# A linear-attention block: the state product by single heads on four 32-column tiles of TensorE

## The chip, the cores and the metric

One core of one Trainium2 chip. The time is the device time of one execution of the whole program, in microseconds; the figure for a kernel is the median of its runs.

## The reference

One transformer block on x of 2048 tokens by 640, all in 32 bits, with scale, shift and gate rows from a condition vector c (`mod = silu(c) @ w_mod`, six rows of 640). What matters here is its first half, attention with 32 heads of 20:

```python
q, k, v = split(h @ wqkv)                      # h: layer norm of x, scaled and shifted
phi(p) = concat(softmax(p @ w_phi), softmax(-p @ w_phi))        # per head, 20 + 20 features
kv  = einsum("bhsf,bhsd->bhfd", phi_k, v)      # the state: 40 x 20 a head, summed over all tokens
z   = einsum("bhsf->bhf", phi_k)               # the sums of k
num = einsum("bhqf,bhfd->bhqd", phi_q, kv)
den = einsum("bhqf,bhf->bhq", phi_q, z) + 1e-6
x   = x + ga * ((num / den) @ wo)
```

The second half is a layer norm and an MLP of 640 by 1728 with squared ReLU, and a second gated residual.

## The kernel before

Tokens are cut into 16 tiles of 128 (`NT`), taken in pairs `j` of 256. Nearly every product of the block is made in three terms of rounded operands (`three`: high by high, high by low, low by high), so a projection of one token tile to 640 columns is 30 matmuls of 128 by 128 by 320 elements. Products whose operands are plain 32-bit numbers, the state product among them, show in the trace as two weight loads and two matmuls each.

*First phase.* `first` folds `w_phi` into the weights of q and k, makes the first modulation rows (`mod_rows2`, line 530: a product with 32 equal columns a tile of the array, on four column tiles) and the first two tiles. Then a loop over t = 2 to 13 runs, for each token tile: `proj("k")`, `do_v`, `do_q`, the softmax numerators (`spread`, `exps`), the norm of k (`k_norm`), the sums of the numerators of q (`q_sums`, `q_chain`), and `do_kv(t - 1)`. `t1` transposes the next pair's normalized tokens for the projections through PSUM banks. `ln_parts` is the layer norm of a later pair, on ScalarE and GpSimd. The order on TensorE is the order written (`by_pe`); on the other engines a planner puts the instructions in order by its estimate of time, and each engine then runs its list in order. `sides` is work that the second half needs: modulation rows (`mod_rows`, `mod_cols`: loads, five multiply-adds on VectorE, then matmuls or transposes) and the output weights (`prep_wo`), advanced by two steps a tile and by eight from t = 11.

*The state.* `do_kv` takes the 32 heads in 11 groups `UN` of three heads (the last of two). The value tile of a group is stationary, 60 columns and one column of ones, so that the state and the sums of k come out together; the features of k stream, 2 x 60 elements. Groups alternate between two 64-column tiles of the array. Each product also holds the cross terms of its three heads, which a mask takes away later. The state lies in a PSUM tile `kvp` of three banks; its third bank and the tile `tp` also serve transposes and small products.

*Between the phases* everything is in the order written on TensorE, VectorE, ScalarE and GpSimd (`order`). The last four token tiles' q is postponed to here as cover (`POSTPONED`). The state is copied to SBUF (`kvs`); `make_z` spreads the sums of k over all partitions with products against a column of the identity (line 735), and copies them to `zb`. From `zb` the denominators follow on VectorE and GpSimd (`e_prod`: lines 831 and 833; `e_recip`; `e_scale`: lines 852 and 857), and `tr_e` transposes the scaled features (line 978). `kv_diags` and `kv_masks` transpose the state and mask it for the first four pairs' `num`; `kv2_mask`, `kv2_pick` and `kv2_turn` make a second arrangement of it for the later pairs. A loop over `j` in 0 to 3 then does the output product (`do_wo`), with jobs hung in at places `EXTRA[(j, place)]`: `ln_next`, `blocks` and `back` (a transpose of blocks through DRAM), `turn` (line 1190), and `both`.

*Second phase.* `group(g)` runs the MLP over groups of 512 tokens: `up_mm`, `up_relu` (line 1394), `up_out`, `down`. MLP weights are loaded and split in high and low by `prep_load`, `prep_hi` (line 1093) and `prep_lo`, in the order `preps`; raw weights wait in rows tagged "s1" (three buffers) up to index 8, then "s1", "s2", "s4" in turn. The later half of the tokens' attention output is filled in behind the MLP of the first two groups.

Of the kernel before, what the change touches and what calls it, by code (L numbers as in the profile page):

```python
# [15 lines left out]
P = 128  # L16
# [11 lines left out]
UN = [(60 * u, 60) for u in range(10)] + [(600, 40)]  # L28
NU = len(UN)
# [14 lines left out]
def kernel(  # L44
# [80 lines left out]
    kvp = psK.tile([P, 3, 512], F32, name="kvp")  # L125
# [22 lines left out]
    vt = [pc.tile([P, NU, 64], F32, name=f"vt{i}") for i in range(2)]  # L148
    mask2 = pc.tile([120, 128], F32, name="mask")
    mask = mask2[:, :64]  # L150
    mask5 = pc.tile([80, 40], F32, name="mask5")
    for v in vt:
        nc.gpsimd.memset(v, 0.0)
        nc.gpsimd.memset(v[:, :, 60:61], 1.0)

    def head_mask(m, rows, n, at):

        m3 = m.rearrange("p (h d) -> p h d", d=DH)
        nc.gpsimd.affine_select(out=m3, in_=m3, compare_op=ALU.is_ge, fill=0.0, base=-at,
                                pattern=[[-DH, n], [0, DH]], channel_multiplier=1)  # L160
        nc.gpsimd.affine_select(out=m3, in_=m3, compare_op=ALU.is_ge, fill=0.0, base=DH - 1 + at,
                                pattern=[[DH, n], [0, DH]], channel_multiplier=-1)

    mtmp = row("s2", "mtmp")[:120, :60]
    nc.gpsimd.memset(mask, 0.0)
    nc.gpsimd.memset(mask[:, :60], 1.0)
    nc.gpsimd.memset(mtmp, 1.0)
    head_mask(mask[:, :60], 120, 3, 0)
    head_mask(mtmp, 120, 3, 60)
    nc.gpsimd.tensor_tensor(mask[:, :60], mask[:, :60], mtmp, op=ALU.add)  # L170
    nc.gpsimd.tensor_copy(mask2[:, 64:], mask)
    nc.gpsimd.memset(mask5, 1.0)
    nc.gpsimd.memset(mtmp[:80, :40], 1.0)
    head_mask(mask5, 80, 2, 0)
    head_mask(mtmp[:80, :40], 80, 2, 40)
    nc.gpsimd.tensor_tensor(mask5, mask5, mtmp[:80, :40], op=ALU.add)


# [80 lines left out]

    def to_cols(acc, dest, nm):  # L260
        ps = [(0, 4, tp(f"mc{nm}")), (4, 1, kvp[:, 2])]
# [23 lines left out]
    def mod_cols(part, dest):  # L285
# [3 lines left out]
        yield  # L289
        yield  # L290
# [3 lines left out]
    def mod_rows(part, dest):  # L294
        for acc in mod_acc(part):
            if acc is None:
                yield
        yield
        yield
        for h in range(2):  # L300
            p = kvp[:, 2] if h else tp(f"mr{part}")
            nc.tensor.matmul(p[:, :HALF], ones, acc[:, h * HALF : (h + 1) * HALF], start=True, stop=True)
            nc.scalar.activation(dest[:, h * HALF : (h + 1) * HALF], p[:, :HALF], AF.Copy)
        yield
# [65 lines left out]
    def t1(j, ds):  # L370
# [3 lines left out]
        for d in ds:  # L374
            b = banks.setdefault(d // 2, kvp[:, 2] if d // 2 == 1 else tp(f"ta{j}_{d}"))
            t_in(XB[j], d, b[:, 256 * (d % 2) : 256 * (d % 2) + 256])
        for d in ds:
            t_out(cols_a, HT[j], d, f"a{j}", banks[d // 2][:, 256 * (d % 2) : 256 * (d % 2) + 256])
# [15 lines left out]
    def do_v(t):  # L394
        p = proj("v", t, ((0, 360), (360, 640)))
        v = vt[t % 2]
        nc.scalar.activation(v[:, 0:6, :60], p[0][:, :360].rearrange("p (g d) -> p g d", d=60), AF.Copy)
        nc.scalar.activation(v[:, 6:10, :60], p[1][:, :240].rearrange("p (g d) -> p g d", d=60), AF.Copy)
        nc.scalar.activation(v[:, 10, :40], p[1][:, 240:280], AF.Copy)
# [22 lines left out]
    def do_kv(t):  # L422
        v, e = vt[t % 2], EK[t]
        for u, (o, n) in enumerate(UN):
            g, c = divmod(u, 2)
            a = 120 * (g % 4)
            nc.tensor.matmul(  # L427
                kvp[64 * c : 64 * c + 64, g // 4, a : a + 2 * n].rearrange("p (s n) -> p s n", s=2),
                v[:, u], e[:, :, o : o + n],
                start=(t == 0 and g % 4 == 0), stop=(t == NT - 1), skip_group_check=True,  # L430
            )
# [47 lines left out]
    def side():  # L479
        ga_b = row("s4", "ga_b")  # L480
        yield from mod_rows(2, ga_b)
        for g in range(NG):
            yield from prep_wo(g, ga_b)
            yield
# [10 lines left out]
    sides = side()  # L495
# [22 lines left out]
    def half(b, h):  # L518
        return kvp[:, b, 256 * h : 256 * h + 256]
# [131 lines left out]
    do_kv(0)  # L651
# [3 lines left out]
    layer1(2)  # L655
    for t in range(2, NT - 2):
# [22 lines left out]
        if not i and turns:  # L679
            t1(j + 1, turns)  # L680
# [8 lines left out]
    for _ in sides:  # L689
        pass  # L690
# [24 lines left out]
    nc.scalar.activation(kvs[:, :480], kvp[:, 0, :480], AF.Copy)  # L715
    nc.scalar.activation(kvs[:, 480:600], kvp[:, 1, :120], AF.Copy)
    nc.scalar.activation(kvs[:64, 600:680], kvp[:64, 1, 120:200], AF.Copy)
# [10 lines left out]
    kv5 = kv_t[:80, 640:760]  # L728
    def make_z():
        for c in range(2):  # L730
            for b, (g0, g1) in enumerate(((0, 4), (4, 6 - c))):
                r = P if c else 64
                a, n = 480 * b, ((480, 200), (480, 120))[c][b]
                p = psA.tile([P, 512], F32, tag="pj", name=f"z{c}_{b}", bufs=4)
                nc.tensor.matmul(p[:, :n], ident[:r, 64 * c + 60 : 64 * c + 61].to_broadcast([r, P]),
                                 kvs[:r, a : a + n], start=True, stop=True)
                m = min(g1, 5) - g0
                for h in range(2):
                    dst = zb[:, h, 120 * g0 : 120 * (g0 + m)].rearrange("p (g c n) -> p g c n", c=2, n=60)[:, :, c]
                    src = p[:, : 120 * m].rearrange("p (g s n) -> p g s n", s=2, n=60)[:, :, h]  # L740
                    if h:
                        nc.vector.tensor_copy(dst, src)
                    else:
                        nc.scalar.activation(dst, src, AF.Copy)
                if g1 == 6:
                    nc.vector.tensor_copy(zb[:, :, 600:640], p[:, 120:200].rearrange("p (s n) -> p s n", s=2))
# [3 lines left out]
    kvt = [None, None]  # L750
# [1001 lines left out]
```

## Time and profile before

| | |
|---|---|
| median of 3 runs | 780.5 us (780.25 to 781.21) |
| profiled execution | 780.53 us, its span 778.8 us |
| TensorE busy | 770.5 us, 99% of the span; weight loads 716.1 us |
| VectorE, ScalarE, GpSimd busy | 552.7, 401.5, 77.5 us |
| granted TensorE clock | full in all 40 slices |
| moved by DMA | 142.31 MB, 183 GB/s over the span |

Matmuls overlap and their ends are modelled, so the busy share of TensorE does not say that it works at its peak; the time from one matmul's start to the next tells more, and the chain of waits tells which engine sets the end in each stage. "PEld" is TensorE's weight load.

### The profile page before, as it was taken

How to read it: one execution, taken by the hardware profiler on the slowest of the kernel's cores; microseconds unless marked ns; L12 is line 12 of the kernel's file. 1: busy time of each engine (PE TensorE's matmuls, PEld its weight loads, DVE VectorE, ACT ScalarE, POOL GpSimd, SP SyncE). 2: the span in 40 equal slices, each digit the busy share in tenths (PEclk: the TensorE clock that was granted, in tenths of full speed). 3: DMA queues.
4: the chain of work that ended last, by engine and by line, in shares of the span. 5: the costliest groups of instructions: out<-in, count | busy, mean ns of one | idle time of the engine just before them, and what ended most of it. 6: DMA issues, size and time to landing. Idle time of an engine off the chain costs nothing.

```text
span 778.8 us, 13323 instructions
## 1 busy us (share of the span) xinstructions
PE 770.5 (99%) x5163; PEld 716.1 (92%) x5163; DVE 552.7 (71%) x917; ACT 401.5 (52%) x789; POOL 77.5 (10%) x181
## 2 busy tenths in 40 slices
PE   9999999999999999999999999999999999999997
PEld 8899999999999988898999999998999999989997
DVE  4499979998888488573968799958935252575544
ACT  4677585765753235755957345332366545433221
POOL 3002000100100112201323010100010000000000
PEclk9999999999999999999999999999999999999999
DMA  9614215634223263467799657996679754145121
GB/s 346 257 35 133 102 69 188 235 103 154 87 86 103 86 205 137 156 204 269 258 307 351 213 194 244 259 369 191 174 245 365 272 171 147 60 142 203 38 82 68
DMA packets 76437, 142.31 MB, mean 183 GB/s; under 512 B 12718, under 2 KB 37422, under 8 KB 76374
## 3 DMA queue, kind: packets, MB, share of 16 engines
q1 hardware_dynamic: 69094, 117.41, 46.2%
q0 software_dynamic: 4096, 16.78, 5.8%
q10 hardware_dynamic: 3184, 7.27, 2.6%
q8 instruction: 40, 0.66, 0.4%
q14 instruction: 23, 0.19, 0.1%
HBM read 98.40 MB, written 42.93 MB: 181 GB/s over the span
## 4 chain that ended last, share of the span: by engine, by line
PE 84%; DVE 6%; DMA 4%; ACT 3%; POOL 2%; issue 1%; SPq 0%; ACTq 0%; DVEq 0%; POOLq 0%
PE up L70 22%; PE acc L70 14%; PE acr L70 9%; PE pv L70 9%; PE pk L70 9%; PE pq L70 8%; PE pwo L70 4%; PE kvp L427 3%; DVE dn L833 1%; DVE scr L831 1%; DMA rw<-in_w 1%; DVE ezb L852 1%; DMA xb<-in_x 1%; DMA sb<-xn 1%; PE foldq L242 1%
## 5 line engine op out<-in xcount | busy, mean ns | idle before, releaser
L70 PE MATMUL up<-h,w 128*128 128x512 f32 (+1 forms) x910 | 197.8, 370 | 1.1 <-ACT r L1394 0.9
L70 PEld LDWEIGHTS up<-h,w 128*128 128x128 f32 x910 | 155.5, 188 | 28.8 <-DVE h L80 1.2
L70 PE MATMUL acc<-w,r2t 128*128 128x384 f32 x656 | 150.7, 336 | 0.0
L70 PE MATMUL acr<-w,r2t 128*128 128x256 f32 x656 | 112.8, 279 | 0.0
L70 PEld LDWEIGHTS acc<-w,r2t 128*128 128x128 f32 x656 | 107.5, 188 | 4.2 <-DVE w L80 0.2
L70 PEld LDWEIGHTS acr<-w,r2t 128*128 128x128 f32 x656 | 105.5, 188 | 0.0
L70 PE MATMUL pwo<-wo,ot 128*128 128x320 f32 (+1 forms) x512 | 79.5, 313 | 0.2 <-DVE xm L1063 0.2
L70 PEld LDWEIGHTS pwo<-wo,ot 128*128 128x128 f32 (+1 forms) x512 | 75.8, 188 | 1.1 <-DVE xm L1063 0.4
L70 PE MATMUL pk<-wk,hT 128*128 128x320 f32 x480 | 75.3, 313 | 0.0
L70 PE MATMUL pq<-wq,hT 128*128 128x320 f32 x480 | 74.0, 311 | 0.4 <-ACT k L403 0.4
L70 PE MATMUL pv<-wv,hT 128*128 128x360 f32 (+1 forms) x480 | 72.8, 309 | 0.0
L70 PEld LDWEIGHTS pk<-wk,hT 128*128 128x128 f32 x480 | 70.6, 188 | 1.8 <-issue 0.6
L70 PEld LDWEIGHTS pv<-wv,hT 128*128 128x128 f32 x480 | 71.5, 188 | 0.0
L70 PEld LDWEIGHTS pq<-wq,hT 128*128 128x128 f32 x480 | 70.6, 188 | 0.9 <-ACT k L403 0.6
L1394 ACT ACTIVATE r<-up,b_t 128x512 f32<-128x512 f32 x52 | 35.0, 680 | 66.9 <-PE up L70 58.9
L80 DVE TENSOR_TENSOR r2t<-r,r2t 128x512 fp32r<-128x512 f32 (+1 forms) x56 | 38.3, 685 | 33.0 <-ACT r2t L1406 30.1
L1405 DVE TENSOR_TENSOR r<-r 128x512 f32<-128x512 f32 x26 | 17.9, 690 | 47.1 <-ACT r L1394 47.1
L80 DVE TENSOR_TENSOR w<-rw,w 128x640 fp32r<-128x640 f32 (+2 forms) x42 | 33.3, 813 | 24.4 <-ACT w L1093 12.9
L1406 ACT ACTIVATE r2t<-r 128x512 fp32r<-128x512 f32 x52 | 32.9, 633 | 22.5 <-DVE r L1405 21.6
L1496 ACT ACTIVATE w<-rw 128x640 fp32r<-128x640 f32 x42 | 30.6, 729 | 26.4 <-DVE rw L1495 24.1
L403 ACT ACTIVATE q<-pq 128x320 f32<-128x320 f32 x32 | 13.8, 438 | 31.5 <-PE pq L70 30.9
L403 ACT ACTIVATE k<-pk 128x320 f32<-128x320 f32 x32 | 13.5, 431 | 29.5 <-PE pk L70 29.4
(248 smaller groups left out, 1078.1 us busy)
## 6 DMA issues: line engine op xcount, KB each, us to landing
rw<-in_w SPq DMA_DIRECT2D x65, 320.0 KB, 3.5
w<-w2d SPq DMA_DIRECT2D x28, 320.0 KB, 4.7
w<-w1d SPq DMA_DIRECT2D x12, 640.0 KB, 6.3
esp<-eq SPq DMA_DIRECT2D x11, 640.0 KB, 4.7
wm<-in_w_mod SPq DMA_DIRECT2D x20, 320.0 KB, 3.6
xb<-in_x SPq DMA_DIRECT2D x8, 640.0 KB, 4.4
el<-esp SPq DMA_DIRECT2D x8, 640.0 KB, 5.4
xx<-in_x SPq DMA_DIRECT2D x16, 320.0 KB, 5.5
```

Of the source, the lines that this page charges most:

```text
L70: nc.tensor.matmul(o, a, b, start=first and i == 0, stop=last and i == len(terms) - 1, skip_group_check=skip,)
L80: (eng or nc.vector).tensor_tensor(out_lo, full, hi.bitcast(F32), op=ALU.subtract)
L242: nc.tensor.matmul(p[g // 3][:, (g % 3) * 120 : (g % 3) * 120 + n], r, bd_t[:n, g * 120 : g * 120 + n], start=True, stop=True,)
L403: nc.scalar.activation(t[:, h * HALF : (h + 1) * HALF], p[h][:, :HALF], AF.Copy)
L427: nc.tensor.matmul(kvp[64 * c : 64 * c + 64, g // 4, a : a + 2 * n].rearrange("p (s n) -> p s n", s=2), v[:, u], e[:, :, o : o + n], start ...
L831: nc.vector.tensor_tensor(z, flat(ET[t]), flat(zb), op=ALU.mult)
L833: nc.vector.tensor_reduce(dn.rearrange("p s h -> p (s h)"), heads(z), axis=AX.X, op=ALU.add)
L852: nc.vector.tensor_tensor(EU[t][:, :1200].rearrange("p (u s h d) -> p s u h d", s=2, h=3, d=DH), ET[t][:, :, :600].rearrange("p s (u h d) ...
L1394: nc.scalar.activation(r, UP[f], AF.Relu, bias=b1_t[:, f : f + 1])
L1405: nc.vector.tensor_tensor(r, r, r, op=ALU.mult)
L1406: nc.scalar.activation(t[:, 0], r, AF.Copy)
L1496: nc.scalar.activation(w[:, 0], raw, AF.Copy)
```

## The change

1. `do_kv` takes single heads: the value tile is 32 columns a head (20 values, one column of ones, the rest zeros), 2 x 20 features stream, and the heads go round the four 32-column tiles of the array. No cross terms arise. The state then fills 360 columns of one PSUM bank instead of 680 in two; `kvp` becomes three separate tiles.
2. `make_z` uses four products, each of 32 rows of the array (four row groups), into four banks. The state is transposed in three blocks instead of six, once for each arrangement. The masks become one number a partition and head, made on GpSimd; one masked product on VectorE (`masked`) repeats a head's state three times.
3. In the loop `do_kv(t - 2)` stands behind the k projection of tile t, where `do_kv(t - 1)` stood at the end; `t1` follows it, three column blocks on even tiles and two on odd ones, before `do_v`. Side work is in two lists, `mods` and `wos`; the matmuls of `mods` wait for an odd tile and stand behind `t1`.
4. `v` is cut 320 and 320, with two copies to SBUF instead of three; modulation rows are cut 384 and 256.
5. The second arrangement's picks move from place (2, 2) to (2, 1), its turn from (3, 2) to (2, 3); `prep_load` puts the raw rows 5 to 8 in "s4".

```diff
-    kvp = psK.tile([P, 3, 512], F32, name="kvp")
+    kvp = [psK.tile([P, 512], F32, name=f"kvp{b}") for b in range(3)]
...
+    def head_mask(m, rows, n, step):
+
+        tmp = mtmp[:rows, :n]
+        nc.gpsimd.memset(m, 0.0)
+        for at in rows_of(n, step):
+            nc.gpsimd.memset(tmp, 1.0)
+            nc.gpsimd.affine_select(out=tmp, in_=tmp, compare_op=ALU.is_ge, fill=0.0, base=-at,
+                                    pattern=[[-step, n]], channel_multiplier=1)
+            nc.gpsimd.affine_select(out=tmp, in_=tmp, compare_op=ALU.is_ge, fill=0.0, base=step - 1 + at,
+                                    pattern=[[step, n]], channel_multiplier=-1)
+            nc.gpsimd.tensor_tensor(m, m, tmp, op=ALU.add)
...
     def do_v(t):
-        p = proj("v", t, ((0, 360), (360, 640)))
...
+        p = proj("v", t)
+        for h in range(2):
+            nc.scalar.activation(vt[t % 2][:, 16 * h : 16 * h + 16, :DH], heads(p[h][:, :HALF]), AF.Copy)
...
     def do_kv(t):
         v, e = vt[t % 2], EK[t]
-        for u, (o, n) in enumerate(UN):
-            g, c = divmod(u, 2)
-            a = 120 * (g % 4)
-            nc.tensor.matmul(
-                kvp[64 * c : 64 * c + 64, g // 4, a : a + 2 * n].rearrange("p (s n) -> p s n", s=2),
-                v[:, u], e[:, :, o : o + n],
-                start=(t == 0 and g % 4 == 0), stop=(t == NT - 1), skip_group_check=True,
-            )
+        for g in range(9):
+            for c in range(4 if g < 6 else 3 if g < 8 else 2):
+                b, i = divmod(g, 3)
+                h, o = 12 * b + 3 * c + i, state(c, b)
+                nc.tensor.matmul(
+                    o[32 * c : 32 * c + 32, :, i], v[:, h], heads4(e)[:, :, h],
+                    start=(t == 0 and g == 0), stop=(t == NT - 1), skip_group_check=True,
+                )
...
+    def sides(n):
+        for _ in range(n):
+            if not held[0]:
+                held[0] = next(mod_steps, "end")
+            elif gated[0]:
+                next(wo_steps, None)
...
     q_chain(0)
-    do_kv(0)
...
+    head_mask(mask_b, P, 3, DH // 4)
+    head_mask(mask5_b, P, 2, DH // 4)
     for t in range(2, NT - 2):
...
-        turns = ((0, 1) if i == 0 else (2, 3, 4)) if j + 1 < NT // 2 else ()
-        if turns and t == NT - 3:
-            t1(j + 1, turns)
+        do_kv(t - 2)
+        if j + 1 < NT // 2 and t > 2:
+            t1(j + 1, (3, 4) if i else range(3))
+        if i and held[0] == "pe":
+            held[0] = next(mod_steps)
+            gated[0] = True
         do_v(t)
+        if t == 2:
+            t1(j + 1, range(3))
...
-        if i and turns and t < NT - 3:
-            t1(j + 1, turns)
...
-        do_kv(t - 1)
-        for _ in range(SIDES[t >= RAWQ]):
-            next(sides, None)
+        sides(SIDES[t >= RAWQ])
...
         to_sb(proj("k", t), PK[t])
+        do_kv(t - 2)
...
-    do_kv(ka - 1)
...
+        ps = [bank("z0"), bank("z1"), bank("z2"), psA.tile([P, 512], F32, tag="pj", name="z3", bufs=4)]
+        for c, p in enumerate(ps):
+            r, n = slice(32 * c, 32 * c + 32), (360, 360, 320, 240)[c]
+            nc.tensor.matmul(p[:, :n], ident[r, 32 * c + DH : 32 * c + DH + 1].to_broadcast([32, P]), kvs[r, :n], start=True, stop=True)
+        for c, p in enumerate(ps):
+            dst = zb[:, :, :480].rearrange("p s (b c n) -> p s b c n", c=4, n=60)[:, :, :, c]
+            put(c % 2, dst, p[:, :240].rearrange("p (b s n) -> p s b n", s=2, n=60))
...
     def kv_diags():
-        kvt[:] = [bank(f"kvt{b}") for b in range(2)]
-        for g in range(5):
...
+        p = KV1["p"] = bank("kvt")
+        for b in range(3):
+            nc.tensor.transpose(p[:120, P * b : P * b + P], kvs[:, 120 * b : 120 * b + 120], ident)
...
-        raw = row(("s1", "s2", "s4")[i % 3] if i > 8 else "s1", f"rw{k}_{f}")
+        raw = row(("s1", "s2", "s4")[i % 3] if i > 8 else "s4" if i > 4 else "s1", f"rw{k}_{f}")
...
-        (2, 1): [lambda: ln_next(1)],
-        (2, 2): [lambda: ln_next(1), lambda: ln_next(1), kv2_mask, kv2_pick],
+        (2, 1): [lambda: ln_next(1), kv2_pick],
+        (2, 2): [lambda: ln_next(1), lambda: ln_next(1)],
...
-        (2, 3): [lambda: back(1)],
+        (2, 3): [kv2_turn, lambda: back(1)],
...
-        (3, 2): [kv2_turn, lambda: (p_hi(), p_lo()), lambda: turn(1)],
+        (3, 2): [lambda: (p_hi(), p_lo()), lambda: turn(1)],
```

More of the change, by code (lines that the diff above doesn't have):

```diff
@@ L147 @@
     rs_q = pc.tile([P, NTA, 2 * H], F32, name="rs_q")
[L148 to L151, printed above, removed]
+    vt = [pc.tile([P, H, 32], F32, name=f"vt{i}") for i in range(2)]
+    mask = pc.tile([120, 3], F32, name="mask")
+    mask5 = pc.tile([80, 2], F32, name="mask5")
+    mtmp = pc.tile([P, 3], F32, name="mtmp")
+    mask_b = pc.tile([P, 3], F32, name="mask_b")
@@ L152 @@
+    mask5_b = pc.tile([P, 2], F32, name="mask5_b")
     for v in vt:
         nc.gpsimd.memset(v, 0.0)
[L154 to L176, printed above, removed]
+        nc.gpsimd.memset(v[:, :, DH : DH + 1], 1.0)
@@ L179, with rows_of @@
+    def rows_of(n, step):
+        return [n * DH * s for s in range(2)] if step == DH else [32 * a + n * step * s for a in range(4) for s in range(2)]
+    head_mask(mask, 120, 3, DH)
+    head_mask(mask5, 80, 2, DH)
     ET_ = mybir.EngineType
@@ L258, in mac, with spare @@
             nc.vector.scalar_tensor_tensor(acc, t, cs[:, k : k + 1], prev, op0=ALU.mult, op1=ALU.add)
+    def spare(nm):
+        return tp(nm), kvp[2]
     def to_cols(acc, dest, nm):
-        ps = [(0, 4, tp(f"mc{nm}")), (4, 1, kvp[:, 2])]
+        big, rest = spare(f"mc{nm}")
+        ps = [(0, 4, big), (4, 1, rest)]
         for c0, n, p in ps:
@@ L297, in mod_rows @@
                 yield
[L298 to L303, printed above, removed]
+        yield "pe"
+        for p, a, b in zip(spare(f"mr{part}"), (0, 384), (384, D)):
+            nc.tensor.matmul(p[:, : b - a], ones, acc[:, a:b], start=True, stop=True)
+            nc.scalar.activation(dest[:, a:b], p[:, : b - a], AF.Copy)
         yield
@@ L477, in prep_wo, with mods @@
             nc.gpsimd.dma_start(w[2 * n : m, 0], w[2 * n : m, 1])
[L479 to L484, printed above, removed]
+    def mods():
+        yield from mod_rows(2, WO["gate"])
         yield from mod_cols(3, cols_b[:, 0:5])
@@ L493, in side, with wos @@
         yield
-    sides = side()
+    def wos():
+        for g in range(NG):
+            yield from prep_wo(g, WO["gate"])
+            yield
+    def sides(n):
[4 more added lines that the diff above has]
+                next(wo_steps, None)
+    mod_steps, wo_steps, held, gated = mods(), wos(), [None], [False]
     def stats(xt, nm):
@@ L518, in half @@
     def half(b, h):
-        return kvp[:, b, 256 * h : 256 * h + 256]
+        return kvp[b][:, 256 * h : 256 * h + 256]
     MR = {}
@@ L683 @@
             q_sums(t - 1)
-        do_kv(t - 1)
-        for _ in range(SIDES[t >= RAWQ]):
-            next(sides, None)
+        if t == 2:
+            WO["gate"] = row("s4", "ga_b")
+        sides(SIDES[t >= RAWQ])
         if t < RAWQ:
             q_chain(t)
-    for _ in sides:
-        pass
+    while held[0] != "end":
+        held[0] = next(mod_steps, "end")
+    sides(2 * NG)
     by_pe.__exit__(None, None, None)
@@ L728 @@
     kv5 = kv_t[:80, 640:760]
+    nc.gpsimd.memset(kv_t[:120, :640].rearrange("p (u n) -> p u n", n=64)[:, :, 60:], 0.0)
     def make_z():
[L730 to L746, printed above, removed]
+        ps = [bank("z0"), bank("z1"), bank("z2"), psA.tile([P, 512], F32, tag="pj", name="z3", bufs=4)]
[5 more added lines that the diff above has]
+            put(c % 2, dst, p[:, :240].rearrange("p (b s n) -> p s b n", s=2, n=60))
+        for c, p in enumerate(ps[:3]):
+            n = 40 if c == 2 else 60
+            put(c % 2, zb[:, :, 480 + 60 * c : 480 + 60 * c + n], p[:, 240 : 240 + 2 * n].rearrange("p (s n) -> p s n", s=2))
@@ L758, in kv_masks, with masked @@
     def kv_masks():
-        for b, (g0, g1) in enumerate(((0, 4), (4, 5))):
+        masked(kvd, kv5, KV1["p"], mask, mask5, 120, 80)
+    def masked(to, to5, p, m, m5, n, n5):
+        nc.vector.tensor_tensor(
+            to.rearrange("p g (c n) -> p (g c) n", n=64)[:, :, :60].rearrange("p u (h d) -> p u h d", d=DH),
+            p[:n].rearrange("p (u n) -> p u n", n=32)[:, :10, None, :DH].to_broadcast([n, 10, 3, DH]),
+            m[:, None, :, None].to_broadcast([n, 10, 3, DH]), op=ALU.mult
+        )
+        for h in range(2):
@@ L807, in kv2_turn @@
+        masked(k[:, :640].rearrange("p (g n) -> p g n", n=P), k[:, 640:], p, mask_b, mask5_b, P, P)
         nc.scalar.dma_start(KVD, k)
```

97 lines of the change are left out of this document (42 added, 55 removed).

## The prediction

> **What bounds the kernel now.** I read the page first, then the chain of waits in order of time, then single tiles, then windows. Busy shares and the two ends of the chain's tally:
>
> ```profile
> span 778.8 us, 13323 instructions
> PE 770.5 (99%) x5163; PEld 716.1 (92%) x5163; DVE 552.7 (71%) x917; ACT 401.5 (52%) x789; POOL 77.5 (10%) x181
> PEclk9999999999999999999999999999999999999999
> PE 84%; DVE 6%; DMA 4%; ACT 3%; POOL 2%; issue 1%; SPq 0%; ACTq 0%; DVEq 0%; POOLq 0%
> ```
>
> TensorE is busy 99% at its full clock, and 84% of the chain is its own instructions. Time leaves this kernel if TensorE's instruction stream gets shorter where TensorE sets the pace, or if one of its few waits goes. The chain, one token tile of the first phase and the phase's end (start, us, what):
>
> ```profile
> 71.65 1.31 PE kvp L427 x22
> 72.96 4.60 PE pk L70 x30
> 77.56 4.42 PE pv L70 x30
> 82.64 4.40 PE pq L70 x30
> 87.04 1.31 PE kvp L427 x22
> ...
> 258.89 2.47 PE kvp L427 x43
> 261.36 2.39 PE pq L70 x15
> 263.75 2.35 PE z L735 x6
> ```
>
> From one state product to the next there are 15.39 us, and k, v, q and the product make 14.73 of it; the rest is six transposes. No wait stands in it, so in this phase a microsecond off the product is a microsecond off the span. The cover for everything on other engines is this stretch:
>
> ```profile
> 57.00:211.50 154.50, 154.50 (x1191) 151.33 (x1188) 137.62 (x183) 104.04 (x230) 17.50 (x30) 1.00 0.38 132
> 135.00:150.40 15.40, 15.40 (x120) 15.12 (x119) 15.40 (x22) 14.05 (x33) 2.10 (x5) 1.00 0.68 253
> 282.00:343.00 61.00, 60.02 (x423) 53.13 (x419) 45.76 (x80) 35.32 (x77) 11.50 (x29) 1.00 0.55 177
> 343.00:367.00 24.00, 22.96 (x142) 20.54 (x141) 12.18 (x22) 12.66 (x23) 2.83 (x5) 1.00 0.67 225
> ```
>
> (Windows: stretch, length, busy of TensorE, its weight loads, VectorE, ScalarE, GpSimd, clock, DMA.) VectorE has 17 us free in 154, but in one tile it is full. After 282 TensorE waits for 1 us in 61, and again 1 us before 367.
>
> **The state product, term 1.** Now 11 products a token tile, each 64 columns wide by 120 elements (the last 80), on two column tiles; each shows as two weight loads and two matmuls, 22 in all. Afterwards 32 single heads, each 32 columns by 40 elements: 64 matmuls and 64 loads, in rounds of four column tiles. The trace has one other product on four 32-column tiles, the modulation row of line 530:
>
> ```profile
> L427 PE MATMUL kvp<-ek,vt x352: 232/266/318, 56.4 to 261.1; 128*64 128x120 f32 x159, 128*64 128x80 f32 x17
> L530 PE MATMUL mrow<-wm,cs x100: 272/273/298, 19.2 to 31.3; 128*32 128x128 f32 x100
> 42.19 1.09 PE kvp L332 x10
> 23.43 0.78 PE mrow L530 x20
> 27.88:27.95 0.07, 0.05 (x4) 0.05 (x8) 1.00 1.24 479
> ```
>
> What is to be seen: ten transposes of 128 elements on the whole array take 1.09 us, 109 ns each, 0.85 ns an element. Durations differ by the same slope (266 at 120, 232 at 80: 34 ns for 40). The 20 matmuls of 128 elements on four tiles take 0.78 us where one after another they would take 2.18. The last line (line 530 alone) shows four of them and eight weight loads begun within 0.07 us. So four tiles run together, and a round costs its elements once: five rounds of 109 are 0.55, leaving 0.23 for filling and draining. The present product fits: ten rounds of 102 and two of 68 are 1.16 of 1.31, leaving 0.15.
>
> The new product has nine rounds, twice: 18 x 40 x 0.85 = 0.61 us. With 0.24 for fill and drain that is 0.85 against 1.31, a gain of 0.46 for 14 tiles, 6.4 us. The last two run as one: 2 x 0.61 + 0.24 = 1.46 against 2.47, 1.0 us. Together 7.4 us.
>
> Bounds. Below: 0.15 of fill gives 0.76, a gain of 8.9. Above: if a round also paid its weight load instead of hiding it, it would add 27 ns (the first matmul of line 530 lasts 298 where the others last 273, about 25): 18 x 61 + 240 = 1.34, no gain. The queue must also feed 128 instructions in that time:
>
> ```profile
> L530 PEldq EVENT_SEMAPHORE  x1: 51/51/51, 24.7 to 24.7; - x1
> L541 PEldq EVENT_SEMAPHORE  x1: 51/51/51, 25.4 to 25.4; - x1
> ```
>
> These are two waits taken by TensorE's sequencer, 0.7 us apart; in the program 20 matmuls of line 530 and 12 of k lie between, 64 instructions with their loads: at most 11 ns each. 128 x 11 = 1.4 us, less what stands in the queue already, so at worst about no gain, and the true rate may be better. I take 0.85, since line 530 is the same form of instruction; both ends stay in the range.
>
> **The order in the loop.** The product of tile t-2 moves behind the k projection, the transposes behind it, the side work's matmuls behind those. The number of switches between 128-wide and narrow tiles stays one in and one out a tile, so I cost it at nothing. VectorE gets 137.6 us of work in what becomes 150 us: still covered, 92%. If it were not, each full tile would lose up to its 0.46. A product now waits for a norm issued two tiles earlier, and the wait's followers on TensorE (transposes, v, q) have that slack. The value cut into 320 and 320 keeps 640 elements; two ScalarE copies replace three.
>
> Masks: GpSimd gets 18 small instructions instead of 16 and two larger memsets before the first statistics, and 66 new small ones behind the first phase.
>
> ```profile
> POOL sma L313 <- ACT junksa L312: 105.7, 6, 25.6
> L508 POOL TENSOR_SCALAR sqa<-mva 128x2 f32<-128x2 f32 x2 | 0.5, 236 | 23.8 <-DVE cols_a L542 17.0 <-DVE mva L507 6.9
> L159 POOL TENSOR_SCALAR_AFFINE_SELECT mask<-mask x2: 214/226/238, 3.6 to 3.8; 80x40 f32<-80x40 f32 x1, 120x60 f32<-120x60 f32 x1
> ```
>
> The first lot has 6.9 us of idle time ahead of it. The second is about 66 x 0.23 = 15 us against idle stretches of up to 25.6; cost nothing. Without that cover a layer norm would come up to 15 us late, about one tile's period; ScalarE, in order, would stand behind it, and TensorE behind ScalarE's copies for some us.
>
> **Sums of k, term 2.** What follows `z` is a chain of VectorE:
>
> ```profile
> 266.53 0.14 DVE zb L742
> 267.10 1.50 DVE scr L831
> 277.47 4.72 DMA el<-esp
> 319.84 1.31 PE te L978 x10
> L744 ACT ACTIVATE zb<-z x4: 214/296/372, 264.8 to 266.4; 128x240 f32<-128x240 f32 x2, 128x60 f32<-128x60 f32 x2
> L742 DVE COPY zb<-z x4: 209/308/408, 265.2 to 266.9; 128x240 f32<-128x240 f32 x2, 128x60 f32<-128x60 f32 x2
> ```
>
> From 267.1 to 319.8 every step is VectorE, GpSimd or a load it released, so TensorE's own savings there (three transposes fewer in `kv_diags`, 0.3) are worth nothing, but an earlier `zb` moves all of it. The columns stay 1280, twice: 2.35 us if the row groups run in turn. Then the last copy (0.41 + 0.2) still ends near 267.0, gain 0.1. If four row groups run together the longest, 360 elements, takes 2 x 0.31 + 0.24 = 0.86, and copies of 0.37 + 0.37 + 0.24 + 0.22 on ScalarE end at 265.8, gain 1.3. No row shows 32-row groups; the nearest is the four column tiles, which do run together: I take 0.8.
>
> **The second state's turn, term 3.** Two mask transposes and three of six others leave TensorE, eight masked picks become plain copies, three ScalarE copies become one masked product on VectorE, and the turn moves from (3, 2) to (2, 3).
>
> ```profile
> 339.81 0.45 PE kvt L801 x4
> 340.28 0.32 ACT kvd L804
> 341.68 0.75 ACT w L1093
> 343.19 0.76 DVE fa_q L1190 x2
> ```
>
> That clears 1.4 us from the chain ahead of the turn at 343.19 (340.28 to 341.68), but that turn also waits for a load. Against it, about 1.2 us of VectorE work (an estimate by its copies above, 408 ns for 240 elements and 209 for 60: one of 600 and two of 60) now stands before the `num_lo` that the next output product waits for. Bounds: a gain of 0.9, most of the 1.4 us, if the load has landed by then, or a loss of 0.8, if two thirds of the new work shows; I take 0.
>
> **The loads, term 4.** `prep_load` moves four raw weight rows from "s1" (three buffers) to "s4".
>
> ```profile
> 355.89 8.97 DMA rw<-in_w
> 364.89 0.74 ACT w L1093
> 365.63 0.58 ACT r L1394
> PE up L70 <- ACT r L1394: 0.9, 1, 0.9
> ```
>
> A load that waits for its buffer until 355.89 lands nine us later; ScalarE, in order, holds a ReLU behind it, and TensorE waits 0.9. With earlier loads this wait should mostly go: gain 0 to 0.9, I take 0.6. Next late would be the load after those four, back on "s1".
>
> **Sum.** 7.4 + 0.8 + 0 + 0.6 = 8.8 us. The profiled execution took 780.53 (span 778.8 and 1.7 around it), the median of the runs is 780.5: the same, so 771.7.
>
> **Rivals.** *Each matmul costs a fixed time, however short.* Place: line 427. By the mean of line 530, 0.78 / 20 = 39 ns, 64 cost 2.50 us: 14 x 1.19 + (5.0 - 2.47) = 19.2 us more, less 1.4 from the other terms: 798. It decides from 1.31 / 64 = 20.5 ns a matmul. For it: a full round of four takes 109 ns there, 27 a matmul, already above that. Against it: that round is exactly as long as one transpose of the same 128 elements, and four begin within 0.07 us. Two pages of the Trainium skill state such a floor: "TensorEngine Tiling (Array Packing)", Performance Considerations, charges any matmul some 60 cycles and advises against tiling a dimension that is already small, and "TensorE: Matmul & The Clock Gate", Part 1, gives about 25 ns from start to start. An estimate by that page: 64 x 25 ns is 1.6 us and the fill on top, some 787 in all; the four starts within 0.07 us speak against a floor that is shared by the tiles, though no run here shows matmuls of 40 elements.
>
> *The weight load isn't hidden at 40 elements* (1.34 a product, above), so that the change doesn't do what it says: 780.5 - 1.4 = 779. For: 34 ns of streaming barely covers 25 to 27 of loading. Against: with 64 columns the load, twice as long, hides under 102.
>
> *VectorE or GpSimd take the pace in the loop.* Side work at two steps a tile meets a shorter period; if half of the 7.4 is lost to waits: 775.4. For: the tile at 135 with VectorE at 15.40 of 15.40. Against: TensorE didn't wait even there.
>
> **How the numbers follow.** The forecast has 0.60, with its own range 768 to 775 (the fast end: 8.9 + 1.3 + 0.9 + 0.9, and the 0.3 of `kv_diags`, is 12.3); half lost to the loop 0.17; hidden load fails 0.10; fixed cost 0.13. What a measurement here can tell from no change is about 0.2%, 1.6 us. Faster: 0.60 + 0.17 + half of the third's 0.10 = 0.82; same 0.05; slower 0.13. The range runs from that fast end, 768, to 779.5, just above the hidden load's failure; it leaves out the fixed cost and a few in a hundred besides.
>
> **What would show it.** A product of 64 matmuls in 0.8 to 0.9 us in the chain, and a mean period of about 14.8 us; `zb` done about 2.5 us after the first `z` matmul begins, 3.3 now; no wait at 365. Wrong if the product takes over 1.3 us, or if TensorE shows waits between k, product and v.

## The result and the profile after

The changed kernel takes 768.6 us (median; 768.5 to 769.3) against 780.9 for the kernel before on the same chip: a ratio of 0.984, 95% interval 0.983 to 0.986, 12.3 us less. The forecast was 771.7 with a range from 768 to 779.5; the direction was right, the gain was sized at 8.8 and came out at 12.3. The changed kernel was measured twice more, beside experiments: 769.6 against 780.9, and 770.4 against 780.4, gains of 11.3 and 10.0. So 12.3 is the largest of three, and what follows is read from the execution that was profiled with it, unless another is named.

The page of the changed kernel: span and instructions, busy times, the granted clock, and the tally of the chain of waits.

```profile
span 766.6 us, 14695 instructions
PE 758.7 (99%) x5827; PEld 706.3 (92%) x5827; DVE 552.2 (72%) x918; ACT 397.8 (52%) x770; POOL 92.5 (12%) x251
PEclk9999999999999999999999999999999999999999
PE 56%; DVE 6%; DMA 1%; POOL 1%; issue 1%; ACT 1%; SPq 0%; DVEq 0%; ACTq 0%; POOLq 0%
```

TensorE has 664 matmuls more and is busy 12 us less, still 99% of a shorter span. VectorE's busy time has not moved (552.7 before), GpSimd has the 15 us of new small masks (77.5 before). The chain is followed back only to 256.71 us here, so its shares say nothing on the first phase; that one is read by tiles and windows.

The state product, first by its tile (duration min/median/max in ns, first and last start in us), then in windows that fit one product, the last pair, and most of the loop (columns as in the windows shown of before):

```profile
L424 PE MATMUL kvp<-ek,vt x1024: 196/202/223, 61.2 to 252.5; 128*32 128x40 f32 x171
120.94:121.71 0.77, 0.76 (x64) 0.72 (x64) 0.00 (x0) 0.00 (x0) 1.00 0.57 233
251.16:252.64 1.48, 1.47 (x128) 1.42 (x128) 0.00 (x0) 0.00 (x0) 1.00 0.04 11
60.00:211.50 151.50, 151.50 (x1682) 148.50 (x1681) 142.88 (x189) 101.92 (x220) 15.26 (x29) 1.00 0.44 147
```

64 matmuls take 0.77 us where 22 took 1.31, and the pair at the end 1.47 where it was 2.47. From one product to the next there are 14.8 us, as the prediction said, against 15.4 before. In the loop TensorE is still busy in 151.5 of 151.5 us; VectorE has come to 94%.

Now the later marks. These rows are of before: the first `up` and the first and last `acc` (the first product of the MLP's second half).

```profile
L70 PE MATMUL up<-h,w x910: 276/392/502, 342.9 to 764.9; 128*128 128x512 f32 x146, 128*128 128x256 f32 x36
L70 PE MATMUL acc<-w,r2t x656: 331/335/524, 354.8 to 774.1; 128*128 128x384 f32 x164
```

And these of after, with the sums of k, VectorE's first step behind them, and the last `te` that TensorE waits for:

```profile
L750 PE MATMUL z<-kvs,ident x8: 361/462/564, 255.0 to 255.4; 32*128 32x360 f32 x4, 32*128 32x320 f32 x2, 32*128 32x240 f32 x2
L839 DVE TENSOR_TENSOR scr<-el,zb x8: 1475/1484/1493, 257.0 to 298.1; 128x1280 f32<-128x1280 f32 x8
309.67 1.31 PE te L986 x10
L68 PE MATMUL up<-h,w x910: 276/392/398, 331.6 to 753.0; 128*128 128x512 f32 x146, 128*128 128x256 f32 x36
L68 PE MATMUL acc<-w,r2t x656: 331/335/524, 344.5 to 762.2; 128*128 128x384 f32 x164
```

Setting the marks against each other shows where the time went:

| mark | before | after | earlier by |
|---|---|---|---|
| last matmul of the state product | 261.1 | 252.5 | 8.6 |
| VectorE's first step behind `zb` | 267.1 | 257.0 | 10.1 |
| that `te` | 319.84 | 309.67 | 10.2 |
| first `up` | 342.9 | 331.6 | 11.3 |
| first `acc` | 354.8 | 344.5 | 10.3 |
| last `acc` | 774.1 | 762.2 | 11.9 |
| span | 778.8 | 766.6 | 12.2 |

Gains come in four places: the first phase (8.6; 8.9 if it is counted from its first modulation columns, which start 0.3 us later here), the sums of k (1.5), the stretch from `te` to `up` (1.1), and the MLP (1.6; 1.1 and 1.5 in the two further executions of this kernel). In one place a microsecond is lost, between the first `up` and the first `acc`. The chain of waits of after leads to it:

```profile
319.49 7.58 DMA xn<-xm
...
329.32 3.45 DMA sb<-xn
332.90 0.78 DVE fa_q L1198 x2
...
339.40 5.25 PE up L68 x26
```

and the list of TensorE's waits from 318 to 372:

```profile
PE up L68 <- DVE h L78: 0.6, 1, 0.6
```

The wait for a load at 365 is gone. A new one stands at the first `up`: `turn(1)` (the `fa_q` transposes) begins 1.26 us after the first `up`, where before it began 0.27 after it (343.19 against 342.92). It waits for the blocks that it turns, which went 7.58 us through `xn` and 3.45 back; the experiments with the loads show that this wait is about half of the loss.

### The profile page after: what moved, and what is told of

Its sections match the earlier page's. It is cut to its first block, busy times and chain, and to the rows that moved or that the text cites. A ratio compares the mean times of both kernels' runs of the same rounds, so it can differ in the third digit from the quotient of the medians.

```text
span 766.6 us, 14695 instructions
## 1 busy us (share of the span) xinstructions
PE 758.7 (99%) x5827; PEld 706.3 (92%) x5827; DVE 552.2 (72%) x918; ACT 397.8 (52%) x770; POOL 92.5 (12%) x251
## 4 chain that ended last, share of the span: by engine, by line
PE 56%; DVE 6%; DMA 1%; POOL 1%; issue 1%; ACT 1%; SPq 0%; DVEq 0%; ACTq 0%; POOLq 0%
PE up L68 24%; PE acc L68 15%; PE acr L68 10%; PE pwo L68 6%; DVE dn L841 2%; DVE scr L839 1%; DMA xn<-xm 1%; DVE ezb L860 1%; PE numa L68 1%; POOL dn L843 1%; PE numc L68 1%; PE numb L68 0%; DMA sb<-xn 0%; POOL dd L846 0%; PE te L986 0%
## 5 line engine op out<-in xcount | busy, mean ns | idle before, releaser
L68 PE MATMUL pv<-wv,hT 128*128 128x320 f32 x480 | 73.8, 311 | 0.0
L78 DVE TENSOR_TENSOR w<-rw,w 128x640 fp32r<-128x640 f32 (+2 forms) x42 | 33.2, 816 | 23.9 <-ACT w L1101 12.4
L1414 ACT ACTIVATE r2t<-r 128x512 fp32r<-128x512 f32 x52 | 32.9, 633 | 22.5 <-DVE r L1413 21.6
```

What stands on the lines that cost most here:

```text
L68: nc.tensor.matmul(o, a, b, start=first and i == 0, stop=last and i == len(terms) - 1, skip_group_check=skip,)
L78: (eng or nc.vector).tensor_tensor(out_lo, full, hi.bitcast(F32), op=ALU.subtract)
L1414: nc.scalar.activation(t[:, 0], r, AF.Copy)
```

## The experiments

Runs of one kernel differ by 0.4 to 2.9 us, once by 4.8, and the traces show two places where kernels that are alike there differ. One is the entry of the MLP's third group, near 580 us, where the wait was nothing in the profiled execution of after and 1.5 us in that of one experiment. The other is the start: the first modulation columns begin anywhere from 21.6 to 22.6 us. So effects of one microsecond are read from one mark to another, ahead of the third group, and the total comes second. From the first modulation columns to the last product, the profiled executions with the changed first phase have 230.4 to 230.6 us, all nine; the three kernels that alter the product or its place are not among them.

**The column tiles one after another**

```diff
-        for g in range(9):
-            for c in range(4 if g < 6 else 3 if g < 8 else 2):
+        for c in range(4):
+            for g in range((9, 9, 8, 6)[c]):
```

> The changed kernel with the two loops of the state product exchanged: column tile outside, heads inside, so that consecutive products fall on the same 32-column tile. Theory A (the column tiles run side by side, a round of four costs its 40 elements once): now each of the 64 matmuls costs its own 40 x 0.85 = 34 ns, a product takes about 2.2 + 0.1 = 2.3 us instead of 0.77, fourteen of them and the pair at the end (4.5 instead of 1.47) add 14 x 1.53 + 3.0 = 24 us: about 793. If in a row on one tile the weight load is not hidden either (61 ns a matmul, 3.9 us a product): about 818. Theory B (the product is shorter because it streams fewer elements and stores no cross terms, whatever the tiles do together): 0.77 us stays, 768.6.

Measured: 790.0 us, ratio to before 1.012 (1.010 to 1.013). One product in the loop and the last pair:

```profile
126.40:128.48 2.08, 2.07 (x64) 2.01 (x64) 0.00 (x0) 0.00 (x0) 1.00 0.31 57
269.57:273.48 3.91, 3.90 (x128) 3.84 (x128) 0.00 (x0) 0.00 (x0) 1.00 0.20 58
```

The same 64 matmuls in another order take 2.07 us: theory A. 14 x 1.30 + 2.43 is 20.6 us, nearly all of the loss against the changed kernel (21.4 on medians). So what makes the change fast is not that the products are smaller and no cross terms are stored: with the tiles in turn the kernel is slower than before. Nor do fewer elements stream, as theory B supposed: there are 2 x (10 x 120 + 80) = 2560 a token tile before, and 64 x 40 = 2560 after, then on two column tiles and now on four. The single starts in the trace stand 36 ns apart on one tile, near the 34 that the prediction's 0.85 ns an element gives; the mean of 32 is lower because at each change of tile the last matmuls of one tile and the first of the next run together. So the weight load stays hidden even on one tile, at 40 elements.

**Twice as many matmuls, half as long**

```diff
+                for s in range(2):
...
-                    o[32 * c : 32 * c + 32, :, i], v[:, h], heads4(e)[:, :, h],
...
+                        o[32 * c : 32 * c + 32, s, i], v[:, h], heads4(e)[:, s, h],
```

> The changed kernel with each head's product cut into its two halves of 20 elements: twice as many matmuls and weight loads (128 and 128 a token tile), the same elements in sum. Theory A (elements set the time: 36 rounds of 20 x 0.85 = 17 ns): 0.6 + 0.1, the product stays at 0.75 to 0.8 us and the kernel at 768.6. Theory B (instructions set it; in the later rounds of a product the changed kernel shows 10.8 ns from one matmul to the next): 128 x 10.8 = 1.4 us, 16 x 0.6 = 10 us more, 778. Theory C (a fixed cost of some 25 ns a matmul that the four tiles share): the 64 matmuls of the changed kernel already contradict it with 0.77 us; 128 x 25 = 3.2 us, 807.

Measured: 782.9 us, ratio 1.002 (1.001 to 1.003). Windows of a product and of the last pair, the waits of TensorE around that pair, and a line of its DMA queues:

```profile
123.29:124.70 1.41, 1.40 (x128) 1.36 (x128) 0.00 (x0) 0.00 (x0) 1.00 0.46 174
259.74:264.30 4.56, 2.88 (x256) 2.75 (x256) 0.00 (x0) 0.00 (x0) 1.00 0.40 143
PE kvp L425 <- issue: 1.7, 1, 1.7
q8 instruction: 1, 0.02, 1.3%
```

1.40 us for 128 is 10.9 ns a matmul, the number of theory B. But its reason, a pace of instructions that all tiles share, isn't what the single starts show. Through most of the product's later part four matmuls start within some 5 ns, and the next four 33 ns later. Near its end, where only three and then two tiles have heads left, groups of three and of two stand 33 and 31 ns apart as well; at a shared pace of 10.9 ns two would take 22. So a tile takes a matmul about every 32 ns, though 20 elements stream in 17. (The trace doesn't name a matmul's tile; this is read from the sizes of the groups.) In the changed kernel the groups of four stand 36 ns apart: halving the elements saves 4 ns of a round and doubles the rounds. There the elements still set the time, but only just, and shorter pieces would gain nothing. Whether the 32 ns are the weight load that goes with every matmul, or a floor of the matmul itself, no run separates.

The last pair, 256 matmuls in a row, took 4.55 us: in the middle TensorE stood for 1.7 us with no engine to wait for, in a stretch in which one packet of instructions was loaded. The 15 matmuls of q behind it then took 3.8 us until `z`, where the changed kernel has 2.4, with a second such packet. The number of these packets follows TensorE's matmuls and loads: 45 for 11654 of them in the changed kernel, 53 for 13702 here. That TensorE waited for instructions is inferred from this, not shown. 14 x 0.63 + 3.1 is 11.9 of the 13 to 14 us lost, and the slow q is 1.4 more.

**The product back at the end of the loop**

```diff
     q_chain(0)
+    do_kv(0)
...
-        do_kv(t - 2)
...
+        do_kv(t - 1)
         if t == 2:
             WO["gate"] = row("s4", "ga_b")
...
-        do_kv(t - 2)
+        if t == ka:
+            do_kv(ka - 1)
```

> The changed kernel with only the order in the loop undone: do_kv(t - 1) at the end of the iteration, do_kv(0) ahead of the loop, the last ones in their old places; the product itself stays as changed. Theory A (the order is worth nothing, as the prediction costed it; the gain of the first phase is the shorter product): 768.6 within 0.5, the copy of the state to SBUF starts at 252.7 within 0.5. Rival (the order carries part of the first phase's gain, or keeps away a wait that the shorter period would bring): 770 or more, with waits of TensorE in front of the products, which then stand one norm closer to their operands.

Measured: 769.9 us, ratio 0.986 (0.984 to 0.988). For each kernel the start of an early group (the first modulation columns) and the last matmul of the state product; before, after, and this one:

```profile
L541 PE MATMUL kvp<-ident,msb x5: 270/271/330, 21.7 to 33.4; 128*128 128x128 f32 x5
...
L552 PE MATMUL kvp<-ident,msb x5: 270/271/328, 22.0 to 33.7; 128*128 128x128 f32 x5
...
L552 PE MATMUL kvp<-ident,msb x5: 270/271/329, 21.6 to 33.4; 128*128 128x128 f32 x5
L424 PE MATMUL kvp<-ek,vt x1024: 202/202/224, 56.4 to 252.9; 128*32 128x40 f32 x171
```

From the one to the other: 239.4 us before, 230.5 after, 231.3 here. So 8.1 of the 8.9 stay with the product in its old place, and its place brings 0.8. (The place of the transposes, the side lists and the cut of the value were not undone.) The order isn't worth nothing; but its worth doesn't come from waits ahead of the products either, as the rival had it: TensorE shows a single one of 0.2 us. TensorE's timeline shows where most of it lies (start, us, what), after, then here:

```profile
126.83 4.56 PE L68 MATMUL pq<-wq,hT 128*128 128x320 f32 x30
131.22 4.56 PE L68 MATMUL pk<-wk,hT 128*128 128x320 f32 x30
...
126.90 4.56 PE L68 MATMUL pq<-wq,hT 128*128 128x320 f32 x30
131.39 0.84 PE L424 MATMUL kvp<-ek,vt 128*32 128x40 f32 x64
```

Where k follows q, a group of q lasts 4.39 us until the next one starts; where the product follows it, 4.49. Over the first phase's 13 groups of q that is 1.1 us, and the transposes, which stand behind k instead of the product here, get 0.6 back. With product and transposes side by side TensorE leaves the projections once an iteration instead of twice.

**Only the rows of the raw weights, in the kernel before**

```diff
-        raw = row(("s1", "s2", "s4")[i % 3] if i > 8 else "s1", f"rw{k}_{f}")
+        raw = row(("s1", "s2", "s4")[i % 3] if i > 8 else "s4" if i > 4 else "s1", f"rw{k}_{f}")
```

> The kernel before with only the rows of the raw weights changed: indices 5 to 8 on the five buffers of s4 instead of the three of s1. Theory A (the wait of TensorE of 0.9 to 1.2 us at 365 comes from a load that waited for its s1 buffer, and goes with more buffers): 779.7, no wait at 365. Rival (the wait goes in the changed kernel only because other work shifted, or the load of the next index is late instead): 780.9, same as before.

Measured: 779.5 us, ratio 0.998 (0.997 to 0.999). The wait of 0.9 us at 365 no longer appears among TensorE's waits, and no other takes its place: theory A. On the medians of this chip (781.2 before) it is 1.6 us, of which that wait is 0.9; from the first modulation columns to the end, the two traces differ by 1.0. In this kernel the rows cost nothing ahead of the MLP: from the first `up` to the first `acc` it has 12.0 us against 11.9.

**The changed kernel once more, and three parts undone beside it**

> The changed kernel once more, unaltered, as the mark for the three runs beside it: 768.6 within 0.5.

Measured: 769.6 us, ratio 0.986 (0.984 to 0.988), 1.0 above the first measurement and beyond the 0.5 expected; one of its five runs took 773.6.

*The sums of k on all rows of the array*

```diff
-            nc.tensor.matmul(p[:, :n], ident[r, 32 * c + DH : 32 * c + DH + 1].to_broadcast([32, P]), kvs[r, :n], start=True, stop=True)
+            nc.tensor.matmul(p[:, :n], ident[:, 32 * c + DH : 32 * c + DH + 1].to_broadcast([P, P]), kvs[:, :n], start=True, stop=True)
```

> The changed kernel with the four products for the sums of k on all 128 rows of the array instead of 32 rows each (same columns, same elements, the rows of the identity outside the group are zero). Theory A (the four row groups run side by side, z takes 0.80 us, and the end of zb sets VectorE's chain): in turn they take 1280 x 2 x 0.85 = 2.2 us, zb ends about 1.2 us later, te and the end move with it: 769.8. Theory B (VectorE's chain has slack behind zb, or the products ran in turn before): 768.6.

Measured: 772.0 us, ratio 0.988 (0.987 to 0.990).

```profile
L750 PE MATMUL z<-kvs,ident x8: 366/448/466, 254.6 to 256.6; 128*128 128x360 f32 x4, 128*128 128x320 f32 x2, 128*128 128x240 f32 x2
L839 DVE TENSOR_TENSOR scr<-el,zb x8: 1480/1484/1491, 257.7 to 298.8; 128x1280 f32<-128x1280 f32 x8
L68 PE MATMUL up<-h,w x910: 276/392/398, 332.3 to 756.2; 128*128 128x512 f32 x146, 128*128 128x256 f32 x36
...
PE up L68 <- ACT h L1223: 1.5, 1, 1.5
```

The eight starts spread over 2.0 us instead of 0.4, VectorE begins 3.1 us after the first of them instead of 2.0, and the first `up`, 75 us later, is still 0.7 us behind that of the changed kernel, though `z` began 0.4 earlier here: theory A, 1.1 us instead of 1.2. The last line is the wait of 1.5 us at the third group's entry, which makes up most of what else this execution loses, and is no part of what the rows of the array do.

*The raw rows back on s1*

```diff
-        raw = row(("s1", "s2", "s4")[i % 3] if i > 8 else "s4" if i > 4 else "s1", f"rw{k}_{f}")
+        raw = row(("s1", "s2", "s4")[i % 3] if i > 8 else "s1", f"rw{k}_{f}")
```

> The changed kernel with the rows of the raw weights 5 to 8 put back on s1. Theory A (the rows took away the wait behind a late load, worth 0.9 to 1.2 us): that wait comes back in the first group of the MLP (f = 4), 769.5 to 769.8. Theory B (the early loads cost as much as they gain, since they share the DMA engines with the blocks that turn(1) waits for, 7.58 us against 6.8 before): the first matmuls of up start without their 1.1 us of waits, the later wait is back, 768.6. Theory C (the rows do nothing): 768.6 with the waits at up unaltered.

Measured: 771.0 us, ratio 0.988 (0.986 to 0.989). Waits from 318 to 372, a piece of the chain, and the first `acc`:

```profile
PE up L68 <- ACT r L1402: 0.7, 1, 0.7
...
332.22 0.75 DVE fa_q L1198 x2
...
344.93 8.74 DMA rw<-in_w
...
L68 PE MATMUL acc<-w,r2t x656: 331/335/524, 343.8 to 762.5; 128*128 128x384 f32 x164
```

The wait behind the late load is back, and the wait at the first `up` is gone: `acc` begins at 343.8 instead of 344.5, and loses it again at 355. Both halves of theory B are there. From the first to the last `acc` there are 418.7 us here and 417.7 in the changed kernel (418.2 and 417.8 in its other two executions): the new rows bring 0.5 to 1.0 us in the MLP and cost 0.5 ahead of it (0.7, less the 0.2 by which this execution is earlier at `up`). The profiled execution, 768.8, was the fastest of the four; the other three took 771.0 to 771.2, so on medians the kernel with the rows back is 1.4 us slower than the changed one beside it, with intervals that overlap.

*The second state's turn back in its old place*

```diff
-        (2, 1): [lambda: ln_next(1), kv2_pick],
+        (2, 1): [lambda: ln_next(1)],
...
-        (2, 3): [kv2_turn, lambda: back(1)],
+        (2, 3): [lambda: back(1)],
...
-        (3, 2): [lambda: (p_hi(), p_lo()), lambda: turn(1)],
+        (3, 2): [kv2_turn, lambda: (p_hi(), p_lo()), lambda: turn(1)],
```

> The changed kernel with the picks back at place (2, 2) and the turn of the second state at (3, 2), ahead of turn(1) on VectorE. Theory A (as the prediction costed it, nothing: turn(1) waits for its blocks until after 332, and the 1.2 us of masked products fit in front of that): 768.6 within 0.3. Rival (the masked products, now on VectorE right ahead of turn(1), come late and push it): up to 1.2 us later, 769.8.

Measured: 769.6 us, ratio 0.986 (0.985 to 0.987). Waits, chain and marks:

```profile
PE up L68 <- ACT h L1223: 0.7, 1, 0.7
PE up L68 <- DVE h L78: 0.7, 1, 0.7
...
331.32 0.69 DVE kvd L777
332.01 0.27 DVE kvd L783 x2
...
334.24 0.76 DVE fa_q L1198 x2
...
L68 PE MATMUL acc<-w,r2t x656: 331/335/524, 345.6 to 764.0; 128*128 128x384 f32 x164
```

The rival: the masked copies stand in front of `turn(1)`, which begins at 334.24 instead of 332.90, and `acc` is 1.1 us later. The first `up` stays where it was (331.7 against 331.6), so the 1.1 us gained ahead of it don't come from these places. The total doesn't tell this apart from the changed kernel.

**The loads behind the blocks**

```diff
...
+    def late_loads(n):
+        with tc.issue_after(BACK[1]):      # the last load of sb, from back(1)
+            p_load(n)
...
-        p_load((1, 2, 2, 4)[j])
+        p_load((1, 2, 2, 0)[j])
...
-        (3, 3): [lambda: both(range(NC), 1), lambda: (p_hi(), p_lo())],
+        (3, 3): [lambda: late_loads(4), lambda: both(range(NC), 1), lambda: (p_hi(), p_lo())],
```

> The changed kernel with the four raw weight rows 5 to 8 kept on s4, but their loads issued behind the loads of blocks 1 (sb) instead of ahead of them. Theory A (those loads share the DMA engines with xn and sb, and that is why turn(1) comes late and TensorE waits at the first products of up): xn<-xm falls from 7.6 us to 5 to 6, the waits at up (0.6 us and two of 0.24) go, no wait at 355 since the rows are still loaded well ahead, 767.6. Theory B (turn(1) is late because its layer norm is late, whatever the loads do): the waits at up stay, 768.6. Theory C (the loads now come too late and the wait behind ScalarE in the first group returns): 768.6 to 769.6.

> As the run before, with two of the four loads ahead and two behind. Theory A: about half of the gain, 768.1, the waits at up about half as long. Theory B: 768.6, the waits unaltered.

> The changed kernel unaltered, as the mark for the two runs beside it: 768.5 to 769.7.

Measured: 769.0 us with all four behind (ratio 0.985, 0.984 to 0.987), 768.7 with two (0.985, 0.983 to 0.986), 770.4 for the changed kernel beside them (0.987, 0.985 to 0.989), more than was expected of it. SyncE's issues, first of after, then with all four behind:

```profile
319.83 0.47 SPq L1091 DMA_DIRECT2D rw<-in_w  x1
323.38 0.33 SPq L1073 DMA_DIRECT2D x<-xm  x1
327.15 2.77 SPq L1188 DMA_DIRECT2D sb<-xn  x4
...
322.25 2.49 SPq L1188 DMA_DIRECT2D sb<-xn  x4
324.85 0.54 SPq L1073 DMA_DIRECT2D x<-xm  x1
325.50 0.37 SPq L1091 DMA_DIRECT2D rw<-in_w  x1
```

```profile
332.23 0.68 DVE fa_q L1205 x2
...
L68 PE MATMUL acc<-w,r2t x656: 331/335/524, 343.8 to 761.6; 128*128 128x384 f32 x164
```

Without the loads in front, `xn` is written 4.9 us earlier (the loads of `sb`, which wait for it, are issued at 322.25), no wait of TensorE is left at `up`, and none returns at 355: theory A, though a part only. `turn(1)` begins just 0.7 us earlier, since now VectorE is not free before. Two loads behind do as much as four, not half. In the traces this is 0.5 us ahead of the third group; on medians 1.4 and 1.8 us, with intervals that overlap.

The kernel before had loads in front of its blocks as well: SyncE issues four there (328.22 to 330.04), four with the rows back on s1, and five in the changed kernel (317.86 to 319.83). With four, or with all of those held back, there are 12.4 us from the first `up` to the first `acc`, with five 12.9 (13.2 and 13.1 in the other two executions of that kernel). So it is the fifth load that costs 0.5 us or a little more; with four VectorE sets the start of the turn.

**And turn(1) ahead of the weight's low part**

```diff
-        (3, 2): [lambda: (p_hi(), p_lo()), lambda: turn(1)],
+        (3, 2): [lambda: turn(1), lambda: (p_hi(), p_lo())],
```

> The kernel with the loads last, and at place (3, 2) turn(1) ahead of the split of one weight row (p_hi, p_lo) on VectorE instead of behind it. With the loads last the blocks have landed some 4 us before turn(1) starts at 332.1, so VectorE's own order sets it: its add (0.86 us) and the low part of the weight (0.73 us) stand in front. Theory A: turn(1) starts 0.7 us earlier, the last 0.5 us that the first products of up lose go, 767.5 to 768.5, and the first down product stands at 343.3 instead of 343.8. Rival (the split weight is late instead, and TensorE or ScalarE waits for it in the first group): no gain or a loss of up to 0.7 us.

Measured: 768.8 us, ratio 0.984 (0.983 to 0.985).

```profile
332.19 0.69 DVE fa_q L1205 x2
...
334.96 0.65 DVE w L78
...
L68 PE MATMUL up<-h,w x910: 277/392/398, 332.1 to 754.4; 128*128 128x512 f32 x146, 128*128 128x256 f32 x36
L68 PE MATMUL acc<-w,r2t x656: 331/335/525, 344.4 to 763.5; 128*128 128x384 f32 x164
```

From the first `up` to the first `acc` there are 12.3 us; with the loads alone it is 12.4 (their first `up` starts at 331.4), and 11.9 before. Theory A holds in its first half and falls in its second. `turn(1)` does begin 0.7 us earlier, 0.1 us behind the first `up` (332.19 against 332.08) instead of 0.8; but the low part of the weight now runs between its transposes and the steps of VectorE that the products of `up` wait for, and these end as late as before. So the last 0.4 us are VectorE's own list: with the loads behind, TensorE takes 1.1 us less than in the kernel before from that `te` to the first `up`, and VectorE from that `te` to the turn only 0.5 less. The kernels with loads behind took 769.0, 768.7 and 768.8 us, the changed kernel 768.6, 769.6 and 770.4: no total here shows them to be faster.

## Why the prediction was right, and where it was off

*The state product, forecast 7.4, measured 8.6 by its rows* (14 x 0.54 + 1.0), 8.1 by the marks with the old order. The mechanism held: rounds of four column tiles cost their elements once, as the serial run shows by losing it, and as the starts 36 ns apart show. Mis-sized was the fill and drain, taken as 0.24 us a product from line 530; 18 x 34 ns is 0.61, so it measured 0.16, close to the 0.15 of the old product, which the prediction kept as its lower bound. The bound of the queue was far off: 128 instructions in 0.77 us are 6 ns each, and the estimate was at most 11.

*The order, forecast 0, measured 0.8.* "The number of switches stays" was the reason for nothing. It counted the switches between wide and narrow tiles; what changed is how often the projections are broken off, once an iteration instead of twice, and a group of q that is followed by k is 0.1 us shorter. So this was a term and not a detail.

*The sums of k, forecast 0.8, measured 1.5* (from the first `z` to VectorE's next step 3.4 us before, 2.0 after). The question left open, whether row groups of 32 run together, has its answer: they do, and that is worth 1.1 of the 1.5. The value between the two bounds was a hedge; the nearest row pointed to the upper one, 1.3. The rest is not tested; the copies to `zb` are seven now and were nine.

*The second state's turn, forecast 0 between a gain of 0.9 and a loss of 0.8.* The sum was right by luck: 1.1 us gained up to the first `up`, 1.0 lost behind it, and neither in the way that was forecast. The gain was to be an earlier `turn(1)`; that began later against `up`, not earlier. What came is TensorE's own: the mask transposes took 0.27 us and are gone, those of the state take 0.25 instead of 0.83, and `numb` follows `numa` 0.28 sooner. The prediction named these transposes and gave them no time here. The loss is `turn(1)` itself, half by the fifth load and half by VectorE's list. "That turn also waits for a load" was said, and the load's own neighbours were not looked at. In the old place the loss is 2.0 (from `up` to `acc` 13.9 us, and 11.9 before).

*The loads, forecast 0.6, bound 0.9.* In the kernel before, the wait of 0.9 us goes whole, 1.6 us on medians. In the changed kernel one load more runs beside the blocks of `turn(1)` and gives 0.5 back. The prediction named as next late the load behind those four; late was another transfer beside them.

What came over the forecast, by the marks: 1.5 in the first phase (8.9 against 7.4), 0.7 at the sums of k, 0.1 at the turn, and 1.0 in the MLP (1.6 against 0.6; by the two further executions 0.5 and 0.9): 3.3 of the 3.5 us. That the result lies next to the fast end of the range, 768, is luck in part: the product didn't reach the 8.9 of that sum, and the order, which was no term of it, made up for it.

*The rivals.* A fixed cost a matmul decides from 20.5 ns; over four tiles the whole time is 12.0 ns a matmul at 40 elements and 10.9 at 20. What is fixed is some 32 ns on one tile, which four tiles spend side by side, and which 40 elements just cover. The Trainium skill's "TensorE: Matmul & The Clock Gate", Part 1, gives about 25 ns from start to start, and "TensorEngine Tiling (Array Packing)", Performance Considerations, some 60 cycles a matmul: across column tiles neither agrees with these 10.9 and 12.0 ns; on one tile the 32 ns between matmuls of 20 elements lie above 25, and no run here tells such a floor from the weight load. At 40 elements the weight load is hidden. VectorE, at 94%, didn't take the pace in the loop: TensorE had no wait there.

## What to carry to other kernels

Narrow products pay when consecutive ones fall on different column or row tiles of the array, and the order of the loop alone decides it: the same 64 matmuls took 0.77 us or 2.07. Cut them no finer than where the elements still last as long as the least time between two matmuls on one tile, some 32 ns here; a piece of 40 elements takes 36. And when a load is made earlier, ask which transfer it now runs beside: one weight load more ahead of the blocks took one stall away and made the next one.

## What the runs showed of the hardware

- On four column tiles matmuls took 12.0 ns on average over 64 with 40 elements, and 10.9 ns over 128 with 20. Groups of up to four, one on each tile, started 36 ns apart with 40 elements and 31 to 33 with 20, however many tiles were in the group. On one tile with 40 elements the starts were 36 ns apart.
- A group of 30 projection matmuls lasted 4.39 us until the next projection started, and 4.49 where 32-column products came next.
- Eight matmuls of 32 rows on four row groups began within 0.4 us; with 128 rows the same ones began over 2.0 us.
- After 183 of 256 matmuls of 20 elements TensorE stood for 1.7 us with nothing to wait for.
- A write of 640 KB took 7.58 us beside five loads of 320 KB, and the loads that wait for it were issued 4.9 us earlier when these came behind.
